# Attention and a spectral gate on one core: fewer sines, integer turns, first evacuations in halves, and a new order of work

## The chip, the cores and the metric

One core of one Trainium2 chip runs the whole program. The metric is the time on the device in microseconds (us), taken as the median over runs of the same kernel. TensorE (PE) multiplies, VectorE (DVE) and ScalarE (ACT) move results out of PSUM and do elementwise work, GpSimd (POOL) does elementwise work on SBUF alone, and SyncE (SP) issues nearly all DMAs.

## The reference

Sliced to what matters; S = 768, D = 64, four batches, eight heads, so the second stage has 512 channels.

```python
scores = scale * np.matmul(q, k.transpose(0, 1, 3, 2))
full_mask = causal                      # heads 0, 2 and 6
stream_mask = causal & (is_sink | in_win)   # the other heads: 4 first keys, window of 64
...
a = np.exp(scores - max) ; a = a / (sum(a) + 1e-09)
x = heads joined(np.matmul(a, v))       # (4, 768, 512)

proj = x @ w_proj                       # three parts: x1, x2, x3
X2 = np.fft.rfft(x2, n=S, axis=1)
H = np.fft.rfft(filter_fft, n=S, axis=0)[None, :, :]
x2_conv = np.fft.irfft(X2 * H, n=S, axis=1)
y = x1 * x2_conv * x3
return (y @ w_out)
```

## The kernel before

**Work units.** The 32 (batch, head) pairs are handled two heads at a time, as 16 pairs numbered n; pairs 4b to 4b+3 make batch b. A pair's causal score matrix has 21 blocks of 128x128. `CHUNKS` (L19) groups them into six chunks; a chunk's scores for both heads fill one pair of PSUM banks, and one ScalarE instruction `ex{n}.{c}` (L593) takes the exponential of the whole chunk. There are four such pairs of banks (slots 0 to 3, the number behind `@` in the order); every matmul stage shares them.

**A pair's path.** `lq`, `lk`, `lv` load q, k, v (SP). `cq`, `ck` (L522) cast to bf16, `cv` (L531) and `vf` (L541) prepare v. For n < 6 PE transposes q and k (`T{n}.{a}`, L550; a is 0 for q, 1 for k) and `E{n}.{a}` (L555) copies the result to SBUF; for later pairs a DMA transposes (`T{n}`, L560). `sc` (L574) makes the scores, as two matmuls on 64 rows each, one a head, side by side on the array. For n < 4, apart from chunks 0 and 1 of pair 0, `sb` (L587) adds a mask bias through the identity; otherwise `mk` (L603) multiplies the exponentials with a mask on DVE. `at` (L612) multiplies with v; `rec` and `nm` normalise; `f0`, `f1` (L634) add and subtract the two halves of the sequence.

**The spectral part.** The Fourier transforms are matmuls with a table `G` of cosines and sines. With the halves folded, even and odd frequencies separate, and G has for each of them (r = 0, 1) three segments: 128 cosines, 128 sines, and a third segment with 64 cosines and 64 sines of the remaining frequencies. `S` (L640) transforms a pair's attention output, `Se` copies it out, `X` (L681) projects with the second third of w_proj, `Xe` copies out, `pa`, `pb`, `pc` multiply with the transformed filter `HAB` (made by `F`, L435, and `H`, L445 and L447), `c` (L742) transforms back with `Gi` (G transposed by a DMA), `ce` and `cv{b}.{cb}.{r}` (L753) put the two halves together. `x1`, `x3` (L717) are the other two projections, `xs` (L725) copies x1 out, `g` and `y` multiply, `o` (L769) multiplies with w_out, `oe` copies out, `st` stores.

**How G is made.** Before: `fcol` (two pieces of 128 frequencies, two of 64), `angle` = fcol * t/768, `turns` = angle plus a large constant (which rounds to whole turns in fp32), `wrap` = rounded turns minus angle, each once per m = 0, 1, 2 over 384 columns; `size` = absolute value; then `sin1`, `cos1` for the first two segments and `sin2`, `cos2` for the third.

**Order.** Nothing is scheduled by the compiler: `ORDER` (L34) is one list of all operations, and each engine executes its own operations in the list's order. A suffix `/v`, `/s`, `/p` says that a copy, cast, or add goes to DVE, ACT or POOL; `@0` to `@3` names the PSUM slot. The list's text is the only place where engines and slots are chosen, so a wait on one engine holds back all that stands behind it on that engine.

Of the kernel before, what the change touches and what calls it, by code (L numbers as in the profile page):

```python
# [9 lines left out]
FP32 = mybir.dt.float32  # L10
BF16 = mybir.dt.bfloat16
I32 = mybir.dt.int32
# [7 lines left out]
    [(0, 0), (0, 1), (0, 2), (0, 3)],  # L20
    [(4, 4), (4, 5), (0, 4), (0, 5)],
    [(1, 1), (1, 2), (1, 3), (1, 4)],
    [(3, 3), (3, 4), (3, 5)],
# [23 lines left out]
sc3.0@3 sc3.3@2 f02/v sb3.0 vf3/v sb3.3 ex3.0 T4.1@0 scales T4.0 F2.0 ck5/p E4.1/v ex3.3 S2.0@3 cq6/p H2.2/s
E4.0/v S2.1 at3.1@2 H2.0/s Se2/v tn2@0 at3.0 H2.1/s te2/v cv4/p sc4.1@3 rec3 lq7 sc4.2@0 nm3 F0.1@1 ex4.2
F0.0 f03/v ex4.1 f13/v tn3@0 cq5/v T5.1@2 H0.0/v T5.0 S3.0@3 te3/v E5.0/s S3.1 H0.2/v E5.1/s x10.0.0@0
H0.1/v Se3/s x10.0.1 H0.3/v x10.1.0@2 H0.4/v xs0.0/s cv5/p lv6 kinds sc4.3@3 sc4.0@1 ex4.3 sc5.1@0 x10.1.1  # L50
ex4.0 mask1 x30.0.0@3 xs0.1/v lk8 ex5.1 x30.0.1 mask0 sc4.5@2 g0.0 sc4.4@1 ex4.5 X0.1.0@0 ex4.4 mask2 mk4.1
sc5.0@3 sc5.2@2 ex5.0 sc5.4@1 mk4.0 X0.1.1 mask6 ex5.2 x10.3.1@3 Xe0.1/v vf5/s x10.3.0 ck6/p F1.1@2 xs0.3/v
ex5.4 F1.0 T6 mask3 sc5.5@3 vf4/v H1.0/s sc5.3@1 cq7/p x30.1.0@0 mk4.2 lq8 ex5.5 x30.1.1 lv7 ex5.3 X0.2.1@3
mk5.2 H1.1/s at4.1@1 mk5.0 H1.2/s X0.2.0 ck7/s mk5.1 g0.1 cv6/s at4.0 T7 Xe0.2/s at5.1@2 mask4 vf6/p rec4
at5.0 nm4 ck8/s sc6.4@3 rec5 sc6.2@0 f04/v ex6.4 lq9 x10.2.0@1 nm5 x10.2.1 lk9 ex6.2 mask7 mask5 sc6.5@2
cq8/p sc6.1@3 xs0.2/v ex6.5 x30.2.0@0 ex6.1 f15/p mk6.2 sc6.0@1 sc6.3@2 T8 x30.2.1 ex6.0 X0.0.0@3 f05/v
ex6.3 g0.2 sc7.3@1 sc7.1@2 mk6.0 ex7.3 sc7.5@0 X0.0.1 mk6.1 ex7.5 tn4 f14/v S4.0@1 ex7.1 cv7/v sc7.4@0
Xe0.0/v tn5 vf7/p S4.1 ex7.4 S5.1@2 Se4/v cq9/p sc7.0@3 sc7.2@0 ex7.0 S5.0 ck9/v at6.1@1 mk7.2 ex7.2 T9
at6.0 mk7.0 Se5/s sc8.4@3 mk7.1 sc8.0@0 hB ex8.0 rec6 at7.0@2 sw0.1 nm6 sw0.0 at7.1 ex8.4 hA f06/v f16/p
sc8.5@0 lv8 sc8.3@1 rec7 ex8.5 S6.0@3 tn6 nm7 ex8.3 sc8.2@0 S6.1 f17/v ex8.2 f07/v tn7 S7.1@1 Se6/v S7.0  # L60
pa0.1 sc9.2@0 Se7/s sc9.4@3 lk11 sc9.0@2 pa0.0 ex9.2 X1.1.1@1 mk8.2 Gi ex9.4 pb0.1 X1.1.0 pc0.1 ex9.0
X1.0.0@0 mk8.1 X1.2.1@3 Xe1.1/s lq10 pa0.2 cv8/v sc8.1@2 sc9.1@1 pb0.2 vf8/p ex8.1 X1.2.0 pc0.2 X1.0.1 lk10
Xe1.2/s x11.1.1@2 ex9.1 mk8.0 x31.1.1@3 pb0.0 ck11/p x11.1.0 mk9.0 lq11 x31.1.0 xs1.1/s at8.1@1 Xe1.0/s g1.1
at8.0 x11.0.0@2 pc0.0 lv9 rec8 x11.0.1 nm8 x31.0.1@3 xs1.0/v f18/p lv10 sc9.5@1 sc9.3@0 ex9.5 x31.0.0 f08/p
cq10/s c0.1.0@1 g1.0 x11.2.1@2 ex9.3 c0.1.1 ck10/s mk9.1 c0.0.0@0 ce0.1/s mk9.2 T10 x11.2.0 cq11/p ce0.0/s
cv0.1.0 c0.3.1@3 xs1.2/s cv0.1.1 c0.3.0 T11 y0.1 x31.2.1@1 cv9/p ce0.3/v x31.2.0 cv0.3.0 vf9/p lv11 S8.1@2
g1.2 lq12 S8.0 c0.0.1 cv10/p cv0.3.1 Se8/s at9.1@1 cv0.0.0 lwo y0.3 sc10.3@2 sc10.2@3 ex10.3 cv0.0.1 at9.0
lk12 vf10/v ex10.2 x30.3.1@0 rec9 nm9 sc10.4@2 sc10.0@3 ex10.4 x30.3.0 y0.0 f19/p c0.2.0@1 ex10.0 g0.3 tn8
c0.2.1 f09/p sc10.5@2 ce0.2/v sc11.4@3 ex10.5 S9.1@0 cv0.2.0 ex11.4 cv11/p S9.0 tn9 cv0.2.1 x11.3.0@2 pa1.1
Se9/s sc11.5@3 y0.2 lk13 sc11.3@1 ex11.5 x11.3.1 vf11/v ex11.3 sc11.1@3 mk11.2 sc10.1@0 ex11.1 o0.1.0@1  # L70
# [12 lines left out]
ck15/s x12.2.0 nm13 o1.1.0@3 T15 xs2.2/s pa2.2 sc14.3@1 sc14.0@0 mk14.2 sc14.2@2 ex14.0 o1.0.0 sw2.0 cv15/v
pb2.1 o1.0.1 ex14.2 o1.1.1 x32.2.1@0 oe1.1/v cv14/p ex14.3 x32.2.0 vf15/p o1.4.0@2 vf14/s st1.1 g2.2 tn13
# [30 lines left out]
def kernel(  # L115
# [13 lines left out]
    nc = tc.nc  # L129
# [709 lines left out]
```

## Time and profile before

| | before |
|---|---|
| runs, us | 199.34, 198.08, 197.48, 197.08, 196.9 (median 197.48) |
| the profiled execution's own time | 199.34 us, its span 197.6 us |
| PE busy | 184.4 us (93%), 1725 instructions |
| DVE busy | 173.1 us (88%), 300 instructions |
| ACT busy | 143.3 us (73%), 183 instructions |
| POOL busy | 46.6 us (24%), 68 instructions |
| granted TensorE clock, mean | 0.988 |
| DMA | 37.31 MB, mean 189 GB/s |

The span is the time from the first to the last profiled instruction. A matmul's row includes the time in which its last columns drain, and the next matmul runs in that time too: consecutive 512-column matmuls start about 0.216 us apart (16 of them take 3.45 us in the chain) but have rows of 0.379 us on average. "Idle" of PE in the profile is counted from the end of such a row, so a wait costs the array about 0.17 us more than its idle time.

### The profile page before, as it was taken

What the parts mean: (1) busy time and instruction counts of PE and PEld (TensorE: products, weight loads), DVE (VectorE), ACT (ScalarE), POOL (GpSimd) and SP (SyncE); (2) the same over time, 40 slices, a digit from 0 to 9 for tenths busy, and PEclk for the clock granted to TensorE, in tenths of its full rate; (3) what the DMA queues carried; (4) which work ended last, traced back from release to release, by engine and by line L of the source; (5) the groups of instructions that cost most, each with busy time, mean ns of one, the idle gap of its engine ahead of it and who ended that gap; (6) DMA issues with size and microseconds to landing.
All of it is one profiled execution on the core that took longest, in us unless ns stands there. A gap on an engine that the chain in (4) does not pass through costs nothing.

```text
span 197.6 us, 4335 instructions
## 1 busy us (share of the span) xinstructions
PE 184.4 (93%) x1725; PEld 104.5 (53%) x1740; DVE 173.1 (88%) x300; ACT 143.3 (73%) x183; POOL 46.6 (24%) x68
## 2 busy tenths in 40 slices
PE   7489989999998999999998999999989999999990
PEld 2236656764473474465643744466537654555540
DVE  7788999898999999998997898989899986968950
ACT  4969998989998898848388769689879524422341
POOL 4243673333023320415731210322030000000000
PEclk9979999999999999999999999999999999999998
DMA  5999999999989968999999789998998221302346
GB/s 172 305 261 314 252 335 213 228 190 233 194 139 205 165 126 178 205 229 214 194 190 185 128 205 231 216 226 212 230 234 258 43 40 36 126 2 88 124 168 257
DMA packets 93782, 37.31 MB, mean 189 GB/s; under 512 B 84162, under 2 KB 89282, under 8 KB 93762
## 3 DMA queue, kind: packets, MB, share of 16 engines
q1 hardware_dynamic: 91650, 34.94, 80.4%
q0 software_dynamic: 2112, 2.10, 6.6%
q8 instruction: 13, 0.21, 0.5%
q14 instruction: 7, 0.06, 0.1%
HBM read 24.64 MB, written 6.29 MB: 157 GB/s over the span
## 4 chain that ended last, share of the span: by engine, by line
PE 60%; DVE 14%; DMA 12%; ACT 7%; issue 2%; POOL 1%; SPq 1%; ACTq 0%; DVEq 0%; POOLq 0%
PE x_ps L717 14%; PE X_ps L681 10%; PE out_ps L769 8%; PE sc L574 6%; PE att L612 6%; DMA qk_f<-in_k_dram 6%; PE S_ps L640 6%; PE c_ps L742 5%; ACT pT L593 4%; DMA v_f<-in_v_dram 4%; DMA qkT<-qk_bf 2%; DVE conv L753 2%; PE sc L587 2%; PE F_ps L435 2%; DVE attn L627 1%
## 5 line engine op out<-in xcount | busy, mean ns | idle before, releaser
L593 ACT ACTIVATE pT<-sc 128x1024 bf16<-128x1024 f32 (+2 forms) x96 | 82.2, 918 | 12.2 <-PE sc L574 9.6
L717 PE MATMUL x_ps<-xT,wproj 128*128 128x384 bf16 x256 | 46.3, 326 | 0.0
L717 PEld LDWEIGHTS <-wproj 128*128 128x128 bf16 x256 | 24.0, 98 | 18.1 <-issue 2.0
L574 PE MATMUL sc<-qkT 64*128 64x512 bf16 (+3 forms) x256 | 27.6, 312 | 2.4 <-DVE x1s L180 1.1
L603 DVE TENSOR_TENSOR pT<-pT,mask 128x1024 bf16<-128x1024 bf16 x37 | 24.9, 700 | 1.1 <-ACT pT L593 1.1
L612 PEld LDWEIGHTS <-pT 128*128 128x128 bf16 x672 | 22.8, 97 | 3.7 <-issue 1.4
L612 PE MATMUL att<-v_aug,pT 128*128 128x65 bf16 x352 | 23.9, 193 | 0.2
L769 PE MATMUL out_ps<-wout,gy 128*128 128x512 bf16 x89 | 23.1, 380 | 0.5 <-DMA wout<-in_moe_w_out_dram 0.2
L681 PE MATMUL X_ps<-wproj,spectrum 128*128 128x512 bf16 x90 | 22.2, 379 | 0.5
L612 PE MATMUL att<-v_far,pT 128*128 128x65 bf16 x320 | 20.7, 193 | 0.0
L574 PEld LDWEIGHTS <-qkT 64*128 64x128 bf16 x256 | 10.3, 94 | 17.1 <-issue 11.8
L742 PE MATMUL c_ps<-Gi,P 128*128 128x384 bf16 x96 | 18.9, 326 | 0.0
L640 PE MATMUL S_ps<-G,halves 128*128 128x384 bf16 x96 | 18.4, 326 | 0.2
L753 DVE TENSOR_TENSOR conv<-evs,c_ps 128x384 bf16<-128x384 f32 x32 | 16.6, 549 | 1.3 <-ACT evs L184 1.0
L182 POOL CAST v_aug<-v_f 128x768 bf16<-128x768 f32 x10 | 8.5, 853 | 36.1 <-DMA v_f<-in_v_dram 36.1
L541 POOL TENSOR_TENSOR v_far<-v_aug,vmask 128x520 bf16<-128x520 bf16 x9 | 10.2, 1133 | 25.0 <-DVE v_aug L180 16.1
L627 DVE TENSOR_TENSOR attn<-att,rec 128x768 bf16<-128x768 f32 x16 | 15.3, 955 | 0.7
L184 ACT COPY o<-out_ps 128x1024 f32<-128x1024 f32 (+1 forms) x10 | 8.9, 886 | 9.3 <-PE out_ps L769 6.9
L182 POOL CAST qk_bf<-qk_f 128x768 bf16<-128x768 f32 x13 | 11.5, 889 | 14.3 <-DMA qk_f<-in_k_dram 10.7
L184 ACT CAST spectrum<-S_ps 128x768 bf16<-128x768 f32 x11 | 8.8, 804 | 8.3 <-PE S_ps L640 8.1
L769 PEld LDWEIGHTS <-gy 128*128 128x128 bf16 x96 | 8.9, 98 | 10.8 <-issue 1.5
L681 PEld LDWEIGHTS <-spectrum 128*128 128x128 bf16 x96 | 8.9, 98 | 10.7 <-issue 1.3
(98 smaller groups left out, 251.3 us busy)
## 6 DMA issues: line engine op xcount, KB each, us to landing
qk_f<-in_q_dram SPq DMA_DIRECT2D x16, 384.0 KB, 5.7
qk_f<-in_k_dram SPq DMA_DIRECT2D x16, 384.0 KB, 5.9
v_f<-in_v_dram SPq DMA_DIRECT2D x16, 384.0 KB, 6.5
out_dram<-o SPq DMA_DIRECT2D x9, 512.0 KB, 3.3
filt<-in_moe_filter_fft_dram SPq DMA_DIRECT2D x1, 1536.0 KB, 9.4
wproj<-in_moe_w_proj_dram POOLq DMA_DIRECT2D x3, 512.0 KB, 9.4
out_dram<-o SPq DMA_DIRECT2D x6, 256.0 KB, 2.5
Xw<-X SPq DMA_DIRECT2D x8, 128.0 KB, 2.6
```

What stands on the lines that cost most here:

```text
L182: nc.gpsimd.tensor_copy(out=out, in_=in_)
L184: nc.scalar.copy(out=out, in_=in_)
L574: nc.tensor.matmul(sc[:, hh, m * 128:(m + cnt) * 128], lhsT=qkT(n)[rows, 1, j * 128:(j + 1) * 128], rhs=qkT(n)[rows, 0, i * 128:(i + cnt) ...
L593: nc.scalar.activation(out=pT(n)[:, :, c, 0:w], in_=held[f"sc.{n}.{c}"][:, :, 0:w], func=AF.Exp, scale=SCALE)
L603: nc.vector.tensor_mul(near, near, which)
L612: nc.tensor.matmul(att[:, hh, 65 * i:65 * i + 65], lhsT=pT(n)[:, hh, c, 128 * m:128 * m + 128], rhs=(v_far(n) if i >= j + 2 else v_aug(n)) ...
L640: nc.tensor.matmul(ps[:, r, 0:HS], lhsT=halves(n)[:, r, m, :], rhs=G()[:, r, m].rearrange("p s f -> p (s f)"), start=(m == 0), stop=(m == ...
L681: nc.tensor.matmul(ps[:, u, :], lhsT=spectrum(b)[:, cc, r, seg * 128:seg * 128 + 128], rhs=wproj()[:, cc, DM:2 * DM], start=(cc == 0), sto ...
L717: nc.tensor.matmul(ps[:, s, 0:HS], lhsT=wproj()[:, cc, part * DM + cb * 128:part * DM + (cb + 1) * 128], rhs=xT(b)[:, cc, s * HS:s * HS + HS],
L742: nc.tensor.matmul(ps[:, r, 0:HS], lhsT=P(b)[:, t, u, ch], rhs=Gi()[:, r, :, seg, :], start=(seg == 0), stop=(seg == 2))
L753: fn(conv[:, half * HS:half * HS + HS], held[f"evs.{b}.{cb}"], held[f"c_ps.{b}.{cb}"][:, 1, 0:HS])
L769: nc.tensor.matmul(ps[:, i % 2, :], lhsT=gy(b)[:, cb, i * 128:(i + 1) * 128], rhs=wout()[:, cb, :], start=(cb == 0), stop=(cb == NC - 1))
```

## The change

1. **Sines.** `fcol`, `turns`, `angle` and `size` shrink from 384 to 256 columns. `sin2` and `cos2` go. The third segment of G is now copied from the first two, in reversed order and with the sign of the position's parity: four operations `far{p}{r}` on DVE, and one operation `signs` (two small POOL instructions) that they read.
2. **Turns.** `angle{m}` goes; `turns{m}` multiplies and writes an int32 tile (the write rounds), and `wrap{m}` multiplies again and subtracts it.
3. **First pair.** `E0.0` and `E0.1` become two halves each (64 of the 128 positions a half, that is the first and the second 384 rows of the sequence).
4. **Chunks.** Block (0, 3) moves from the first chunk to the fourth: the first has three blocks, the fourth four.
5. **Order.** `ORDER` is replaced as a whole: 1001 operations become 1003, and engines, slots and positions are chosen anew.

```diff
 CHUNKS = [
-    [(0, 0), (0, 1), (0, 2), (0, 3)],
+    [(0, 0), (0, 1), (0, 2)],
     [(4, 4), (4, 5), (0, 4), (0, 5)],
     [(1, 1), (1, 2), (1, 3), (1, 4)],
-    [(3, 3), (3, 4), (3, 5)],
+    [(3, 3), (3, 4), (3, 5), (0, 3)],
...
-    turns = C("turns", [128, NM, HS], FP32, "P")
+    turns = C("turns", [128, NM, 256], I32, "P")
...
-        @op(f"angle{m}")
-            vp().tensor_scalar(out=angle()[:, m], in0=fcol(), scalar1=tfrac()[:, m:m + 1], scalar2=None, op0=ALU.mult)
         @op(f"turns{m}")
-            vp().tensor_scalar(out=turns()[:, m], in0=angle()[:, m], scalar1=MAGIC, scalar2=None, op0=ALU.add)
+            vp().tensor_scalar(out=turns()[:, m], in0=fcol(), scalar1=tfrac()[:, m:m + 1], scalar2=None, op0=ALU.mult)
         @op(f"wrap{m}")
-            nc.vector.scalar_tensor_tensor(out=angle()[:, m], in0=turns()[:, m], scalar=MAGIC,
-                                           in1=angle()[:, m], op0=ALU.subtract, op1=ALU.subtract)
+            nc.vector.scalar_tensor_tensor(out=angle()[:, m], in0=fcol(), scalar=tfrac()[:, m:m + 1],
+                                           in1=turns()[:, m], op0=ALU.mult, op1=ALU.subtract)
...
+    @op("signs")
+        for p in range(2):
+            nc.gpsimd.tensor_scalar(out=signs()[:, p:p + 1], in0=par(), scalar1=4.0 * p - 2.0, scalar2=1.0 - 2.0 * p,
+                                    op0=ALU.mult, op1=ALU.add)
+    for p in range(2):
+        for r in range(2):
+            @op(f"far{p}{r}")
+                near = G()[:, r, :, p, 1:65] if r == 0 else G()[:, r, :, p, 0:64]
+                vp().tensor_scalar(out=G()[:, r, :, 2, 64 * p:64 * p + 64], in0=near[:, :, ::-1],
+                                   scalar1=signs()[:, p:p + 1], scalar2=None, op0=ALU.mult)
...
-                @op(f"E{n}.{a}")
-                    copy(qkT(n)[:, a].rearrange("d (p t) -> d p t", t=NT),
-                       held[turned(n, a)][:, a, 0:S].rearrange("d (t p) -> d p t", t=NT))
+                for half in range(2 if n == 0 else 1):
+                    @op(f"E{n}.{a}.{half}" if n == 0 else f"E{n}.{a}")
+                        rows = slice(64 * half, 64 * half + 64) if n == 0 else slice(0, 128)
+                        copy(qkT(n)[:, a].rearrange("d (p t) -> d p t", t=NT)[:, rows],
+                             held[turned(n, a)][:, a, 0:S].rearrange("d (t p) -> d p t", t=NT)[:, rows])
```

The opening of the new order, and two later pieces that the prediction speaks of:

```
mblank fcol0 lk0 tcol quarter table blank0@0 fcol1 tfrac lq0 ident turns1/v lret turns2/v par sin0 lk1
turns0/v wrap2 lq1 wrap0 lq2 wrap1 lk2 sin1 size ck0.1/p lv0 ck0.0/v blank1@1 cos1 lv2 ones0 heads0 T0.1@0
cq0.1/v cq0.0/s parb code0 E0.1.0/s T0.0@1 ck1/p unit E0.1.1/s blank2@2 E0.0.0/v code1 heads1@0 E0.0.1/v
T1.1@3 lk3 sc0.0@2 heads2 sc0.4@1 E1.1/v code2 sc0.1@0 ex0.0 bias0 ex0.1 sc0.5@3 bias1 sc0.3@2 cq1/v sb0.3
sb0.4 bias2 ex0.3 T1.0@0 mask01 mask00 sb0.5 ck2/p E1.0/v lq3 ex0.4 sc0.2@2 lv1 sb0.2 signs bias3 sc1.5@0
lfilt ex0.2 sc1.1@1 vmask sb1.1 cq2/v sb1.5 ex0.5 mk0.0 sc1.4@2 lq4 sb1.4 ex1.1 cv0/v sc1.2@3 sb1.2 bias6
far10/v ex1.5 sc1.3@1 bias4 bias5 ex1.2 T2.0@0 vf0/v sb1.3 ck3/p T2.1 far00/v lk4 ex1.4 at0.1@3 lv3 cq3/p
...
x30.2.1 lk9 f14/v mk5.2 ex6.5 sc6.4@1 lq9 sc6.2@0 vf7/v ex6.4 at5.1@3 ck8/p g0.2 at5.0 ex6.2 sc6.0@1 rec5
...
```

How many operations change engine between the two lists (DVE, ACT, POOL in each line: before, then after):

| operation | DVE | ACT | POOL |
|---|---|---|---|
| `xs` (x1 out of PSUM) | 6, 1 | 10, 15 | |
| `ce` (first half of the inverse) | 8, 6 | 8, 10 | |
| `oe` (output) | 5, 3 | 10, 12 | |
| `Xe` | 2, 4 | 10, 8 | |
| `Se` | 5, 4 | 11, 12 | |
| `E` (q, k transposed; the first pair's are halves after) | 9, 7 | 3, 7 | |
| `f0`, `f1` | 23, 20 | | 9, 12 |
| `ck` | 5, 3 | 6, 2 | 6, 12 |
| `cv` (cast of v) | 5, 2 | 1, 5 | 10, 9 |
| `vf` | 5, 5 | 2, 1 | 9, 10 |
| `te` | 3, 4 | 1, 0 | |

## The prediction

> **What bounds the kernel now.** I read the busy times and the slices first, then the stretches, the chain, and last the waits of PE.
>
> ```profile
> PE 184.4 (93%) x1725; PEld 104.5 (53%) x1740; DVE 173.1 (88%) x300; ACT 143.3 (73%) x183; POOL 46.6 (24%) x68
> PE   7489989999998999999998999999989999999990
> PEclk9979999999999999999999999999999999999998
> ```
>
> PE is busy in every slice from the third to the last but one. The slice with clock 7 is the exception: from 12.05 to 15.47 us the granted clock was one half. The chain says the same: from 9.64 us on it is mostly PE, and PE's last matmul ends at 193.2. So the end is PE's own work from 9.64 on, plus the places where PE starts a matmul later than it could. Adding up matmuls in the order of the list (columns at the spacing that free stretches show: 0.216 us for 512, 0.163 for 384, 0.031 for 65) and comparing with their real starts, PE is 8.8 us behind its own work at 15.5 us, 9.2 at 22.9, 10.5 at 39, 12.9 at 107.5 and 14.6 at the end. The opening costs 8.8 us, and all the rest only 5.8.
>
> ```profile
> 8.76 0.82 POOL L182 CAST qk_bf<-qk_f 128x768 bf16<-128x768 f32 x1 [5.49 <-DMA qk_f<-in_k_dram]
> 9.64 0.51 PE L550 MATMUL qkT_ps<-identity,qk_bf 128*128 128x128 bf16 x6 [2.29 <-POOL qk_bf L182]
> 11.90 0.69 PE L587 MATMUL sc<-bias,identity 128*128 128x128 bf16 x4 [0.81 <-DVE bias L396]
> 10.62 1.02 ACT L593 ACTIVATE pT<-sc 128x1024 bf16<-128x1024 f32 x1 [0.91 <-PE sc L574]
> 12.21 1.51 ACT L593 ACTIVATE pT<-sc 128x512 bf16<-128x512 f32 x2 [0.56 <-PE sc L587]
> 14.24 5.20 ACT L593 ACTIVATE pT<-sc 128x768 bf16<-128x768 f32 x6 [0.52 <-PE sc L587]
> ```
>
> The first scores wait in PE's queue behind T1.1, which waits for the second pair's k. Then the second and fourth exponentials wait for the mask bias.
>
> ```profile
> PE sc L574 <- DVE x1s L180: 1.1, 2, 0.7
> PE sc L574 <- DVE xT L180: 0.7, 1, 0.7
> PE sc L574 <- DMA qkT<-qk_bf: 0.5, 1, 0.5
> 39.35 1.46 PE L435 MATMUL F_ps<-fold,G 128*128 128x512 bf16 x5 [0.25 <-ACT HAB L447]
> ```
>
> These are five later waits (columns of the first three: idle in all, times, longest; the fourth is an instruction with its idle). Measured from start to start, so with the 0.17 us of overlap that each loses, they cost 0.82 and 0.60 (x1s at 63.2 and 107.5), 0.83 (xT at 28.9), 0.67 (qkT at 145.9) and 0.41 (39.35): 3.3 of the 5.8 us.
>
> **The sines and turns.** Before: three passes of 384 columns, some 0.33 to 0.47 us apart, then four sines on ACT (0.85, 0.51, 0.60, 0.92). After: turns and wraps of 256 columns, six instead of nine, and two sines. On DVE that saves some 1.6 us before 6 us, on ACT 1.1. Both at zero: behind them T1.1 still waits for lk1, fourth in SP's list before and after, which landed at 8.71. Nothing reads G before the first transform at 25 us. Without that cover they would be worth up to 1.7 us (the table load ahead of the first exponential ended at 9.71 and could end near 8.0). Added are four `far` on DVE; the nearest rows, 128x128 in 0.175 us and 128x384 in 0.35, give 0.7 to 1.4 us in all, in a stretch (15 to 25 us) where DVE has 9.2 of 10 us busy. I take 1.0; `cv0`, `vf0` and `nm0` stand behind them, and the walk below pays for it. `signs` is two POOL instructions: between 0.12 us (a small memset) and 1.71 (L342, the only arithmetic of POOL on the int32 tile), so 0.2 to 3.4. I take 3.4. POOL is busy only 1.9 of the 5 us from 15 to 20; queued behind are ck3, cq3 and cv1, which by the upper price end at 17, 18 and 19 us, and T3 and at1 come at 19.7 and 22. Hidden; uncovered it is 1 to 2 us.
>
> **Halves and chunks.** E0.0 and E0.1 took 0.95 each, in series on DVE, done at 8.72; now two engines share them and the first scores need only the first halves. Hidden by the same T1.1; zero. The first exponential is 0.82 instead of 1.02, the fourth chunk's the reverse; zero in sum. The fourth chunk's scores become two runs. In a run of scores the next pair of another width starts 9 ns late, so 16 more pairs cost 0.15 us.
>
> **The opening, walked by hand.** Behind T1.1 (9.64 again) the list puts two chunks that need no bias. ex0.0 starts at 10.4, ex0.1 follows at 11.2 and covers the wait for code2, heads2 and the bias: sb0.3 runs at 11.8, ex0.3 at 12.2, and ACT has no more gaps (before: 0.56 and 0.52). Following PE, DVE (0.95 for E1.1 and E1.0, 0.27 a bias, 0.69 mk0.0 and vf0) and ACT (0.93 for 1024 columns) to the first `at`, it starts at 18.05 us after 9.9 us of listed work, against 17.75 after 8.8. That is 8.15 behind instead of 8.9: **-0.75 us**. If PE is granted half clock from 12 to 15.5 again, it and not ACT sets the pace there and -0.3 is left; with k1 late by 1 us, +0.5. If the clock stays full in both, -1.0.
>
> **Switches between scores and other matmuls.** This speaks against the change, and is easily overlooked, since columns and matmuls otherwise stay.
>
> ```profile
> 16.69 0.50 PE L587 MATMUL sc<-bias,identity 128*128 128x128 bf16 x4
> 17.13 0.39 PE L574 MATMUL sc<-qkT 64*128 64x512 bf16 x2
> 17.45 0.39 PE L587 MATMUL sc<-bias,identity 128*128 128x256 bf16 x2
> ```
>
> The scores at 17.13 use 64 rows each, side by side, so 512 columns take 0.216 us; the next matmul on 128 rows starts 0.32 after them, 0.1 late. Four bias matmuls before them need 0.33 and the scores start 0.44 later. Over the trace the median is 95 ns on leaving and 98 on entering: 0.193 a visit. The list before visits scores 46 times, the new one 52. Two of the six fall into the opening, which other waits pace; four cost 0.8: **+0.8 us** (0 if they fall into waits, 1.2 at most).
>
> The Trainium skill, TensorEngine Tiling (Array Packing), Key Properties, says that a change of tiling mode drains TensorE, while changing the tile within a mode does not; it names no price, and the rows above agree with it on both halves.
>
> **What leaves DVE.** Counting engine changes with the page's means (xs 0.95 against 0.80, ce 0.55 and 0.48, oe and Xe 1.21 and 1.02, f 0.45 against 0.96 on POOL, casts 0.55 to 0.59 against 0.84 to 0.89), DVE loses 12.4 us, ACT gains 3.5, POOL 8.5. ACT has room (73%). For the five waits I looked up what now stands between producer and user in the list. x1s of 63.2 and 107.5 goes to ACT behind one or two exponentials, with 1.8 and 2.2 us of matmuls to cover it. te0 no longer stands behind f11 and f01 (the pair took 1.92 us) but behind fold1, with 0.65 to spare. H2.2 moves to DVE, and the bank's next user comes 4.7 us after its matmuls; the evictions and what ACT does between them take 3.3. T15 has 6.1 us of matmuls from its place to its first score, instead of 4.1. All five go: **-3.3 us**.
>
> Others will form; the list is new everywhere. Over the whole list, the reuses of a PSUM slot whose cover (matmuls between the slot's last use and its next) exceeds its eviction by under 0.3 us number 47 in the old list and 44 in the new, so neither is looser there. DMA transposes have 4.4 us at least, where 4.1 was late and 4.5 was not. Bounds: nothing new, and 5.8 anew, all that PE lost after the opening. As DVE has 12 us more room, I take half of what was removed: **+1.6 us**.
>
> POOL's work costs DVE something. `halves` at 26.48 (f11 and f01) shows it: f11 alone took 1.65 us beside POOL's v_far, against 0.35. Over all groups DVE's rows exceed their undisturbed times by 7.1 us, 0.15 for each us of POOL; 8.5 more makes 1.3, so DVE's relief is 11 and not 12.4. That is inside the +1.6.
>
> SBUF — State Buffer, Who interferes with whom, speaks harder against it: a DVE instruction with two SBUF inputs and a GpSimd instruction that reads SBUF exclude each other, and the second waits for the first to end. An estimate by that page: if each of ten added POOL instructions blocked one of DVE for its whole 0.9 us, 9 of the 12.4 us would be gone, the waits would come back in full, and the sum would be about +0.2. This trace shows one full block (f11) and many POOL instructions without, so the measured share decides.
>
> **Sum.** -0.75 + 0.8 + 0.15 - 3.3 + 1.6 = -1.5 us. The profiled execution took 199.34 us, 1.74 of them outside its span of 197.6, and is the slowest of the five; the same sum there gives 197.8. Against the median of 197.48 it is **196.0**.
>
> **Rivals.**
> 1. *All of it holds and nothing new forms*: -3.1, with the full clock -3.35: 194.2. For it: DVE's relief. Against: the nearly equal number of tight slots.
> 2. *The waits only move*: +3.3 in place of +1.6 makes +0.2: 197.7. For it: PE is at 97% between 20 and 160 us, so any list leaves a few us.
> 3. *DMA transposes come late* (slower). The stretch is pairs 8 to 14: T8, T9, T10, T12 and T14 have 5.1 to 5.3 and 4.4 us to their scores, the transposes' median from issue to landing is 4.7, single ones need more, and SP's one queue holds back all behind a wait. If they land 1 us later than before, four are late by 0.5 to 1 us and the loads behind them too: +3.5 on top of rival 2's +0.2: 201.2; from 0.7 us later on it decides (199.5). For it: DMA engines are near full until 155 us. Against: T15's only loss before was 0.67.
> 4. *The opening doesn't move* (half clock, k1 later): -1.5 + 0.75 to +1.25 = 196.7 to 197.2.
>
> **How the numbers follow.** My case (195.0 to 197.0) 0.40, rival 1 0.20, rival 2 0.13, rival 3 0.20, rival 4 0.07. A change of 1% (195.5 and 199.5) is about what a measurement of this kernel can tell from none. Faster by more: rival 1 and about half of my case, 0.41. Slower by more: rival 3 and a bit of rival 2, 0.22. Within: 0.37. The range runs from rival 1's end, 194.0, to 199.6, where rival 3 begins to decide; my case's own is 195.0 to 197.0.
>
> **What would show it.** Right: ex0.0 near 10.4 and no gap on ACT before 16 us; DVE near 160 us busy, POOL near 58; no PE wait on x1s at all; 52 visits of scores; PE's idle sum smaller though its work is 1 us more. Wrong: lk1 landing elsewhere than 8.7; new PE waits of over 3 us in sum, on ACT's xs or on qkT; many DVE rows stretched beside POOL; the clock halved for longer.

## The result, and the profile after

The new kernel is slower: 201.02 us median over 43 runs (198.29 to 207.75), the old one 197.67 over 80 (196.44 to 201.25). The ratio is 1.0097, 95% interval 1.0078 to 1.0116. This ratio, like every ratio below, leaves out slow executions, those more than 1.5% above the same kernel's fastest; for the new kernel these are 19 of the 43, all from 201.3 us up, so its median, 1.7% above the old one, holds a loss that the ratio does not. Forecast were 196.0 us and a range of 194.0 to 199.6.

The profiled execution took 203.48 us, 201.7 of them its span. Its busy times, PE's slices and its granted clock:

```profile
PE 186.9 (93%) x1756; PEld 105.0 (52%) x1772; DVE 165.8 (82%) x284; ACT 147.6 (73%) x188; POOL 58.4 (29%) x77
PE   7987998999999999999759999999989999999990
PEclk9999999999999999999996999999999999999999
```

DVE is 7.3 us less busy than before, ACT 4.3 and POOL 11.8 us more. PE's row is full as before, except for a hole in slices 20 and 21 (5 us a slice, so from 96 to 106 us), and behind it the clock drops for one slice. The hole is named by PE's waits (us in all, times, longest):

```profile
PE sc L580 <- DMA qkT<-qk_bf: 4.1, 3, 2.2
PE att L618 <- DVE v_far L545: 1.1, 1, 1.1
PE sc L580 <- DVE qkT L180: 0.9, 2, 0.5
PE S_ps L646 <- DVE qkT L180: 0.5, 1, 0.5
PE att L618 <- DVE xT L180: 0.4, 1, 0.4
```

Nothing waits for x1s any more. In its place stand scores that wait for the DMA transpose of q and k, and four waits that the old kernel did not have or had elsewhere. The timeline shows the first line's two great instances, with the issue of w_out's load by POOL ahead of them (start, duration, what, idle before and releaser), then the chain with the transposes in it, then two windows with the granted clock:

```profile
95.41 0.81 POOL L423 DMA_DIRECT2D wout<-in_moe_w_out_dram  x1
99.30 0.56 PE L580 MATMUL sc<-qkT 64*128 64x384 bf16 x6 [1.33 <-DMA qkT<-qk_bf]
105.26 0.39 PE L580 MATMUL sc<-qkT 64*128 64x384 bf16 x4 [2.21 <-DMA qkT<-qk_bf]
```

```profile
95.35 9.86 DMA qkT<-qk_bf
105.21 0.05 issue
...
142.69 6.94 DMA qkT<-qk_bf
```

```profile
99.00:105.20 6.20, 3.74 (x29) 1.56 (x29) 3.46 (x6) 4.11 (x5) 2.98 (x3) 1.00 1.38 158
105.20:109.20 4.00, 3.94 (x19) 1.25 (x20) 2.52 (x4) 2.30 (x3) 1.10 (x1) 0.57 1.37 221
```

T11, the transpose of pair 11, was issued at 95.35 and took 9.86 us to land; in the execution profiled before it took 4.2 us (94.82 to 99.02). In these window rows the first numbers are the length and PE's busy time, and the 0.57 near the end is the granted clock: after the wait PE ran for some 3.4 us at half clock (3.4 of 4.0 us at a half and the rest at full make 0.57). The Trainium skill, TensorE: Matmul & The Clock Gate, Part 1: The HAM clock gate, gives about 3.4 us as the window in which PE's idleness is judged. The half clock lasts as long here (3.41 us, from 105.70 on), but PE's longest idle time ahead of it was 2.2 us, shorter than that window.

w_out's load was issued at 95.41, 0.06 us after T11, and landed at 106.22. In the old list `lwo` stands on POOL behind `cv9`, `vf9` and `cv10`; in the new list these casts have moved away and only `cq11` and `cv11` stand ahead. So it starts 1.3 us sooner, at T11's own time.

The opening of the new kernel, and of one that has the old order up to 93 us (before_lwo_with_T11, below):

```profile
6.91 0.82 POOL L182 CAST qk_bf<-qk_f 128x768 bf16<-128x768 f32 x1 [1.83 <-DMA qk_f<-in_k_dram]
8.61 9.12 ACT L599 ACTIVATE pT<-sc 128x768 bf16<-128x768 f32 x11
15.97 1.32 DVE L545 TENSOR_TENSOR v_far<-v_aug,vmask 128x520 bf16<-128x520 bf16 x1
17.33 0.19 PE L618 MATMUL att<-v_far,pT 128*128 128x65 bf16 x1 [1.13 <-DVE v_far L545]
```

```profile
7.36 0.82 POOL L182 CAST qk_bf<-qk_f 128x768 bf16<-128x768 f32 x1 [4.08 <-DMA qk_f<-in_k_dram]
9.75 5.10 ACT L593 ACTIVATE pT<-sc 128x1024 bf16<-128x1024 f32 x6
15.36 0.68 DVE L541 TENSOR_TENSOR v_far<-v_aug,vmask 128x520 bf16<-128x520 bf16 x1
15.85 0.25 PE L612 MATMUL att<-v_aug,pT 128*128 128x65 bf16 x3
```

The second pair's k lands at 6.9 and 7.3 us here, not at the 8.71 of the execution that the prediction was made from. The new order's first exponential comes 1.70 us after k's cast begins (8.61 and 6.91) and ACT has no gap in 9.12 us, both as foretold; but the first product with v begins at 15.95 us, no sooner than the old order's 15.85. By the prediction's listed work (9.9 us ahead of it against 8.8) PE is 6.1 us behind there and not 7.0, with k cast 0.45 us sooner; then it waits for `vf0`, 1.3 us from start to start, and at 23 us it is 7.4 us behind in both profiles.

### The profile page after: what moved, and what is told of

It is laid out like the page before. It is cut to its first block, busy times and chain, and to the rows that moved or that the text cites. A ratio compares the mean times of both kernels' runs of the same rounds, so it can differ in the third digit from the quotient of the medians.

```text
span 201.7 us, 4388 instructions
## 1 busy us (share of the span) xinstructions
PE 186.9 (93%) x1756; PEld 105.0 (52%) x1772; DVE 165.8 (82%) x284; ACT 147.6 (73%) x188; POOL 58.4 (29%) x77
## 4 chain that ended last, share of the span: by engine, by line
PE 63%; DMA 13%; DVE 10%; ACT 5%; SPq 3%; issue 2%; POOL 2%; POOLq 0%; DVEq 0%
PE x_ps L723 17%; PE X_ps L687 10%; PE out_ps L775 9%; DMA qkT<-qk_bf 8%; PE att L618 7%; PE sc L580 7%; PE c_ps L748 6%; PE S_ps L646 4%; ACT pT L599 3%; DMA v_f<-in_v_dram 3%; DMA qk_f<-in_k_dram 2%; PE sc L593 2%; DVE bias L400 1%; PE F_ps L439 1%; DVE v_far L545 1%
## 5 line engine op out<-in xcount | busy, mean ns | idle before, releaser
L723 PE MATMUL x_ps<-xT,wproj 128*128 128x384 bf16 x256 | 47.4, 330 | 0.0
L580 PE MATMUL sc<-qkT 64*128 64x128 bf16 (+3 forms) x288 | 28.3, 293 | 5.4 <-DMA qkT<-qk_bf 4.1
L609 DVE TENSOR_TENSOR pT<-pT,mask 128x1024 bf16<-128x1024 bf16 x37 | 28.5, 784 | 2.5 <-ACT pT L599 2.5
L182 POOL CAST qk_bf<-qk_f 128x768 bf16<-128x768 f32 (+1 forms) x19 | 18.8, 1001 | 32.3 <-DMA qk_f<-in_k_dram 18.1
L640 POOL TENSOR_TENSOR halves<-attn 128x384 bf16<-128x384 bf16 x12 | 12.4, 1042 | 33.0 <-DVE attn L633 33.0
L646 PE MATMUL S_ps<-G,halves 128*128 128x384 bf16 x96 | 19.3, 332 | 0.6 <-DVE qkT L180 0.5
L545 POOL TENSOR_TENSOR v_far<-v_aug,vmask 128x520 bf16<-128x520 bf16 x10 | 11.6, 1160 | 20.8 <-ACT v_aug L184 17.8
L184 ACT COPY o<-out_ps 128x1024 f32<-128x1024 f32 (+1 forms) x12 | 10.5, 880 | 7.2 <-PE out_ps L775 7.2
L737 DVE TENSOR_TENSOR gy<-x1s,x_ps 128x768 bf16<-128x768 bf16 x12 | 11.3, 949 | 4.8 <-PE x_ps L723 2.4
L184 ACT CAST x1s<-x_ps 128x768 bf16<-128x768 f32 x15 | 11.9, 806 | 4.3 <-PE x_ps L723 4.3
```

What stands on the lines that cost most here:

```text
L182: nc.gpsimd.tensor_copy(out=out, in_=in_)
L184: nc.scalar.copy(out=out, in_=in_)
L580: nc.tensor.matmul(sc[:, hh, m * 128:(m + cnt) * 128], lhsT=qkT(n)[rows, 1, j * 128:(j + 1) * 128], rhs=qkT(n)[rows, 0, i * 128:(i + cnt) ...
L609: nc.vector.tensor_mul(near, near, which)
L646: nc.tensor.matmul(ps[:, r, 0:HS], lhsT=halves(n)[:, r, m, :], rhs=G()[:, r, m].rearrange("p s f -> p (s f)"), start=(m == 0), stop=(m == ...
L723: nc.tensor.matmul(ps[:, s, 0:HS], lhsT=wproj()[:, cc, part * DM + cb * 128:part * DM + (cb + 1) * 128], rhs=xT(b)[:, cc, s * HS:s * HS + HS],
```

## The experiments

Several kernels were timed beside the same runs of the old one. Its medians were 198.05 us beside after_again, after_lwo_early, before_lwo_with_T11 and open_after_rest_before; 197.88 beside before_17_visits, before_new_code, before_four_moves and open_after_rest_before2; 197.87 beside after_47_visits, after_47_vf0_early, before_new_sines and before_new_chunks; 197.94 beside the other three. "Lag" is PE's start less the work listed ahead of it, as in the prediction, each visit to the 64-row scores counted with its 0.193 us.

### w_out's load out of the way, or into it

The new kernel again, then the same with `lwo` moved up behind `cq9`; and the old list with `lwo` at T11's time.

```diff
  (new list)  ... mk7.2 ex7.1 sc7.0@2 cq9/p
+ lwo
  ... cv11/p g1.2 S8.0@2 lk12
- lwo
```
```diff
  (old list)  ... c0.3.0 T11 y0.1 x31.2.1@1 cv9/p
+ lwo
  ce0.3/v ... cv10/p cv0.3.1 Se8/s at9.1@1 cv0.0.0
- lwo
```

> The changed kernel once more, for a second profile. In the first one (span 201.7 us) PE stood still for 1.5 us at 99.3 and 2.4 us at 105.3, each time for a DMA transpose of q and k (T10, T11): T11 was issued at 95.35 us and landed at 105.21, while the load of w_out was issued at 95.41. Theory A (w_out's load overtakes T11 on the shared DMA engines): the waits vary with the race between the two; in an execution near 198.5 us the T11 wait is under 1 us, in one above 201 it is 2 us or more. Rival B (the new order loses evenly: switches between scores and other matmuls, waits on DVE and ACT): the wait for T11 is alike in fast and slow executions, and the difference is spread over many places.

> The changed kernel with one word of the order moved: the load of w_out (lwo) follows cq9 on POOL, some 28 us earlier than before. Theory A: T11 lands 4 to 5 us after its issue, the waits at 99 and 105 us shrink to under 1 us in sum, the time falls by 2 to 4 us to 196.5 to 198.5, and the spread of the runs becomes like that of the kernel before (some 2 us instead of 9). Rival B: time and spread stay within 0.5 us of the changed kernel's, about 199.5 to 201.

> The kernel before with one word of the order moved: lwo goes ahead of vf9 and cv10 on POOL, so that it is issued near 95 us, with T11, and not at 96.7. Theory A: T11 lands 8 to 10 us after its issue instead of 4.2, PE waits 2 us or more for the scores of pair 11, and the time rises by 1 to 4 us, with a wide spread. Rival B: nothing but w_out's own arrival changes; within 0.5 us of the kernel before.

Measured: the new kernel 203.98 us (199.18 to 205.5, ratio 1.010 with 1.004 to 1.016); with the early load 200.11 (199.3 to 201.16, 1.0114 with 1.0076 to 1.0152); a second time 200.68 (197.99 to 201.19, 1.0095 with 1.005 to 1.0139). The old list with the load at T11's time took 199.22 (197.15 to 204.15, 1.0027 with 0.9993 to 1.006); five of its twelve runs lie between 200.25 and 204.15, where the old kernel's 17 end at 198.85.

> The kernel of after_lwo_early once more, beside the one with the old chunks. If what is left over before is PE's own work for the six added visits (1.17 us in the order's sum, against waits that are level with before): 199.0 to 200.2, ratio 1.006 to 1.012. If it is waits: PE's lag on its own work at the end differs from the first profile's 12.95 us by more than 1 us, and the ratio goes with it.

PE's waits on the transposes, first new kernel again, then with the early load, first and second profile:

```profile
PE sc L580 <- DMA qkT<-qk_bf: 3.9, 2, 2.9
```
```profile
PE sc L580 <- DMA qkT<-qk_bf: 0.3, 1, 0.3
```
```profile
PE sc L580 <- DMA qkT<-qk_bf: 2.1, 2, 1.2
PE c_ps L748 <- DMA Gi<-G: 0.6, 1, 0.6
```

And the old list, where the load beside T11 makes a chain step of it:

```profile
93.06 7.72 DMA qkT<-qk_bf
```

From issue to landing, in nine of the profiles, in us (a star where w_out's load was issued within 1.3 us of it):

| kernel | pair 9's transpose (T9) | T11 | w_out's load issued |
|---|---|---|---|
| before | 3.7 | 4.2 | 96.70 |
| before_new_sines | 3.7 | 4.1 | 95.70 |
| before_17_visits | 3.7 | 4.1 | 96.40 |
| before_lwo_with_T11 | 3.7 | 7.7* | 93.31 |
| before_four_moves | 8.1* | 4.3 | 65.92 |
| after | 3.7 | 9.9* | 95.41 |
| after_again | 3.8 | 11.0* | 94.87 |
| after_lwo_early | 9.0* | 5.2 | 67.03 |
| after_lwo_early_again | 7.7* | 5.2 | 67.11 |

Where T11 took 4.1 or 4.2 us the load was in flight too, but issued 1.9 us or more behind it (1.7 in open_after_rest_before2, where T11 took 3.9). Issued up to 0.3 us behind a transpose, or up to 1.3 ahead of it, the load doubles it, whichever transpose it meets, in both lists. In the new list T9, with the early load, lands nearly in time (at 76.11 in the first profile, its first score starts at 76.15, 0.4 us late); T11, with the later load beside it, does not. So this part is shown: the collision made the new kernel's spread (up to 207.75 us, at most 201.19 in the 18 runs with the early load). How much of the median it makes is less certain: 3.9 us with six runs each (203.98 less 200.11), but the 201.02 of all 43 runs is only 0.3 to 0.9 above the two medians with the early load. The 1% of the ratio stays with the early load. That load is not clear of the transposes, though: it meets T9 in both profiles, which cost PE 0.4 us in the first, and no run of the new list had it clear of both. So what part of the 1% is still w_out's load is open.

### Old and new halves of the list joined

The new list as far as `tn3`, then the old. In the first version pair 5's k was loaded behind pair 6's, as the new list has it, while the old rest needs it first.

```diff
  (new list to tn3, then the old)  second version:
- ... at0.0 E2.1/v ex1.3 sc1.0@2 ones2 lk6 ... F2.1@3 lk5
+ ... at0.0 E2.1/v ex1.3 sc1.0@2 ones2 lk5 ... F2.1@3 lk6
```

> The new order up to tn3 (about 37 us), then the old order for the rest, with all of the change's code (sines, integer turns, halves, chunks). If the opening is a gain that the rest gives back (theory A, and the opening of the first profile, where the first attention matmuls start at 15.95 us instead of 17.75): 1 to 2 us faster than the kernel before, 195.5 to 196.5. If the code changes or the opening are at fault (rival C): as slow as the changed kernel, 199 to 201. If the gain of the opening is used up by DMA, since loads come no earlier: within 0.5 us of the kernel before.

> The new order up to tn3, then the old one, as in open_after_rest_before, but with the loads of pair 5's and pair 6's k exchanged: in that run PE waited 4.5 us at 43.5 us for pair 5's k, which the new order loads after pair 6's and the old order needs early. With the seam mended, if the new opening gains nothing (its first attention matmul at 16 us, the same as the old order's where the second pair's k lands at 7.3 us): within 0.8 us of the kernel before. If the new opening gains: 1 to 2 us faster. If it costs: 1 us slower or more, with PE's waits before 40 us.

Measured: 204.74 us (201.2 to 208.04), with PE waiting 4.5 us at 43.5 us for that k, an artefact of the seam that tells nothing; then 200.28 (198.76 to 201.91), ratio 1.0105 with 1.0062 to 1.0147. In the second profile k landed at 8.19 us. An opening worth -0.75 in an unchanged rest would have given 197.1. But the new chunks are in this old rest as well, where they alone cost 1.6 us (below): pair 13's transpose takes 6.4 us here and PE waits 1.25 us for it at 131.49. Beside before_new_code, which has the same code with the old opening, it is 0.9 us faster (200.28 and 201.21), with intervals that overlap. With the seam and the late k also in the number, it shows no gain of the opening and excludes none; what tells of the opening is the lag in the profiles above.

### Visits of the 64-row scores

Seventeen more visits in the old list, by moving 18 matmul words between the last two chunks of a group (three of the 18 shown); later, five fewer in the new one, by moving five words beside their other halves.

```diff
  (old list)
- sc5.1@0 x10.1.1 ... sc7.2@0 ex7.0 S5.0 ... sc13.4@0 cv13/p at12.0
+ x10.1.1 sc5.1@0 ... S5.0 sc7.2@0 ex7.0 ... at12.0 sc13.4@0 cv13/p
```
```diff
  (new list, lwo behind cq9)
- sc7.1@0 S4.0    S5.0@1 ... sc7.2@2 S5.1    S9.0@0 ... sc11.3@3 S9.1    x11.3.0@1 ... x11.3.1
+ S4.0 sc7.1@0    sc7.2@2 S5.0@1 S5.1    S9.0@0 S9.1 ... sc11.3@3    x11.3.0@1 x11.3.1
- x30.3.1@3 ... sc10.3@2 x30.3.0
+ x30.3.1@3 x30.3.0 ... sc10.3@2
```

> The kernel before with 18 words moved: behind pair 3, a matmul stage that follows a group of scores is put between the group's last two chunks, so that PE visits the 64-row scores 63 times instead of 46. The same matmuls, banks and engines. Theory S (each visit costs PE 0.19 us, and PE is the bound, so the change's six more visits cost what is left of its loss without the transposes' delay, 1.2 us): 17 more visits cost 3.3 us, 200.5 to 202 beside 198. Theory W (the switches fall into PE's waits, since other engines hold it up anyway): under 0.8 us.

> The new kernel with w_out's load moved up behind cq9 (as in after_lwo_early, whose time was 200.11 us and 1.0114 of before), and with five matmul words moved next to their other halves (S4.0, S5.0, S9.1, x11.3.1, x30.3.0), so that PE visits the 64-row scores 47 times and not 52. Theory A, the visits cost their switches: 18 words moved in the old order cost 2.3 to 2.4 us for 17 visits more, 0.14 us each; five fewer give -0.7 us: about 199.4, ratio 1.008, and the work of PE in the order's own sum falls by about 0.9. Theory B, the visits are hidden by waits of other engines, and what the 17 cost was their changed evictions: no change, 200.1, ratio 1.011. Theory C, a word moved from its place breaks its cover: 0.5 to 1 us slower, with a new PE wait on S4, S5, S9 or x11.3 in the trace.

Measured: 17 more visits take 200.15 us, ratio 1.0121 (1.0103 to 1.0139): 0.0121 x 197.88 = 2.4 us, 0.14 us a visit. Six come to 0.85 us, against the 0.8 of the prediction. Five fewer in the new list did not give the 0.7 back: 200.8 us, 1.0131 (1.0085 to 1.0177). Its waits, which all stand in the profile of after_47_vf0_early as well, name what stood in the way:

```profile
PE sc L580 <- ACT pT L599: 1.4, 4, 0.7
PE xt_ps L659 <- DVE attn L633: 1.0, 1, 1.0
PE sc L580 <- DVE X L180: 0.8, 1, 0.8
```

Where two chunks of scores more stand in a row, PE reaches the bank that ACT's exponential still holds: this wait was 0.3 us, once, in the profile with 52 visits. In the old list a visit costs its switches; in the new one the stage that PE visits from also covers the exponentials, and the price of its visits alone was not measured there.

### Each code change by itself, in the old list

All code changes at once, with `signs` and `far` in places of mine between 17 and 23 us; then sines and turns alone, chunks alone, halves alone.

```diff
  (old list)
- angle0/v angle1/v angle2/v sin2 cos2   E0.0/v   E0.1/v
+ E0.0.0/v E0.0.1/v   E0.1.0/v E0.1.1/v
+ signs (behind cq3)  far10/v (bias6)  far00/v (cv1)  far01/v (f00)  far11/v (E3.1)
```

> All of the change's code (256 columns, integer turns, sines copied, halves, chunks) in the old order; signs and the four far put at their earliest places, the rest unmoved. Theory A (the code is neutral, the loss is in the new order): within 0.8 us of the kernel before. Rival C (the code itself costs, by far and signs in the full stretch from 15 to 25 us, or by two-run chunks): 1 to 2 us slower, with DVE behind from 16 us on. Rival G (the code itself gains, and the order lost more than that): 0.8 us faster or more.

> The old order, chunks and first evacuations, with the sines and turns of the change alone: six passes of 256 columns in place of nine of 384, two sines in place of four, signs on POOL and four far on DVE between 17 and 23 us, where DVE is full. All code changes together cost 3.3 us in the old order (201.21, ratio 1.0164). Theory A, the sines are what costs it (far delay qkT of the third pair, attn and the normalisation behind them, which waited 0.7 to 1.2 us at 16.3, 23.2 and 27.3 us): +2 to +3.3 us, ratio 1.010 to 1.016. Theory B, the prediction's: far 1.0 us on DVE against 1.1 to 1.6 us less work ahead of 6 us, all hidden: within 0.5 us of before, ratio 0.998 to 1.003.

> The old order and sines, with block (0, 3) moved from the first chunk to the fourth, and nothing else. For every pair the first exponential is 0.2 us shorter and the fourth 0.2 us longer, and the fourth chunk's scores become two runs. Theory A, the prediction's: 16 more pairs of matmuls cost 0.15 us: ratio 1.000 to 1.002. Theory B, the old order was laid out for a short fourth chunk (sc3 stands late in most pairs, ahead of the product with v): the exponential that is 0.2 us longer is waited for in each of 16 pairs, up to 0.1 to 0.2 us each: +1.5 to +3 us, ratio 1.008 to 1.015. If both before_new_sines and this one stay under 1.004, the halves of the first pair (two instructions in place of one on DVE) are left as the cause, or the 3.3 us are a sum of waits that need all three edits.

> The old order, chunks and sines, with the first pair's two evacuations in two halves each, all on DVE. In the old order the sines alone cost 0.95 us and the chunks alone 1.43 us by the medians (0.8 and 1.6 by the ratios), all code changes together 3.3. Theory A, the halves cost the rest: two more DVE instructions in series ahead of the first scores, +0.2 to +0.9 us, ratio 1.001 to 1.004. Theory B, T1.1's wait for the second pair's k covers them, as the prediction has it: ratio 0.998 to 1.002, and the 3.3 us hold about 0.9 that only the three together make.

| in the old list | median, us | ratio (interval) |
|---|---|---|
| all code changes | 201.21 | 1.0164 (1.0128 to 1.0201) |
| sines and turns | 198.82 | 1.0041 (1.0009 to 1.0073) |
| chunks | 199.30 | 1.0083 (1.0058 to 1.0109) |
| halves | 198.14 | 1.0021 (0.9988 to 1.0055) |

The three add up to 1.45% of the 1.64%, which is inside the intervals. The chunks are the largest, though the array's work is the same. Of their 1.6 us the profile shows this wait in the timeline, and the step of the chain ahead of it:

```profile
128.85 0.72 PE L574 MATMUL sc<-qkT 64*128 64x384 bf16 x10 [1.39 <-DMA qkT<-qk_bf]
```
```profile
122.24 6.56 DMA qkT<-qk_bf
```

This is pair 13's transpose. With the new chunks in the old list it takes 6.4 to 6.7 us in all four profiles that have them, 4.7 to 5.1 in the six that don't. Why a fourth exponential that is 0.2 us longer lengthens this transfer was not found. Then the same edit undone in the new list:

```diff
  (new list, lwo behind cq9)
-    [(0, 0), (0, 1), (0, 2)],
+    [(0, 0), (0, 1), (0, 2), (0, 3)],
-    [(3, 3), (3, 4), (3, 5), (0, 3)],
+    [(3, 3), (3, 4), (3, 5)],
```

> The new kernel with w_out's load behind cq9, and block (0, 3) back in the first chunk. In the old order moving that block alone cost 1.6 us (199.30, ratio 1.0083), and its trace showed 1.56 us of it as one wait of PE for the DMA transpose of pair 13. Theory A, the chunks carry a price of their own in any list: about 1.6 us less than after_lwo_early, 198.5, ratio 1.003. Theory B, the price was the old list's, which was laid out for the old chunks, and the new list is laid out for the new: no gain, 200.1 or up to 1.5 us more, ratio 1.011 to 1.019, with new waits in the opening, where the first exponential now needs the second halves of the first pair's evacuations.

Measured: 201.76 us (199.64 to 204.01), ratio 1.0165 (1.0109 to 1.0222), beside 1.0095 with the new chunks. So the same edit costs 0.8% in the old list, and in the new one it saves about 0.7%, with intervals that overlap. The chunks have no price that holds in both lists, and undoing them does not bring back what remains of the loss.

### Taking waits away

Three of the prediction's five waits (the two on x1s and the one on xT), treated in the old list by three moves, with w_out's load moved up as the fourth; and `vf0` ahead in the new one.

```diff
  (old list)
- xs0.2/v   xs1.3/v   f11/v tn0@3 ex2.3 lv5 f01/v sb2.0 te0/v   cv0.0.0 lwo
+ xs0.2/s   xs1.3/s   tn0@3 te0/v f11/v ex2.3 lv5 f01/v sb2.0   cq9 lwo
```
```diff
  (new list, lwo behind cq9, 47 visits)
- cv0/v sc1.2@3 sb1.2 bias6 far10/v ex1.5 sc1.3@1 bias4 bias5 ex1.2 T2.0@0 vf0/v
+ cv0/v vf0/v sc1.2@3 sb1.2 bias6 far10/v ex1.5 sc1.3@1 bias4 bias5 ex1.2 T2.0@0
```

> The kernel before with five words changed: w_out's load after cq9 instead of after cv10; te0 (and tn0) ahead of f11 and f01 on DVE; xs0.2 and xs1.3 on ACT. It takes away the waits that the prediction had counted (xT 0.8 to 1.1 us, x1s 0.8 and 0.6 us) and w_out's transfer from the stretch of T10 and T11. If waits add up on PE: 1.5 to 2.5 us faster than the kernel before, 195.5 to 196.5. If they only move, as they did in the changed kernel: within 0.6 us.

> As after_47_visits, and vf0 stands directly behind cv0 on DVE, ahead of bias6, far10, bias4 and bias5. In the new kernel the first matmul on v waited 1.1 to 1.4 us for vf0 (start to start), which the prediction had not seen. Theory A, the opening's delay is carried to the end: 1.3 us less than after_47_visits, about 198.1 and level with before. Theory B, waits only move: something a few us later (E2.1, the third pair's scores, xT at 33 us or qkT at 35 us) waits instead; within 0.4 us of after_47_visits. Under B PE's lag on its own work at 35 us is again about 8.7 us; under A it is about 7.4.

Measured: the four moves take 199.08 us, ratio 1.0046 (1.0026 to 1.0066). Of the waits on xT and x1s (1.09 and 0.72 us in before_lwo_with_T11) 0.35 is left. All of PE's waits from 14 to 75 us, with the four moves and then in before_lwo_with_T11 (the old order up to there):

```profile
PE sc L574 <- ACT pT L593: 0.3, 1, 0.3
PE F_ps L435 <- ACT HAB L447: 0.2, 1, 0.2
PE sc L574 <- DVE qkT L180: 0.2, 1, 0.2
```
```profile
PE sc L574 <- DVE xT L180: 0.9, 1, 0.9
PE sc L574 <- DVE x1s L180: 0.6, 1, 0.6
PE F_ps L435 <- ACT HAB L447: 0.2, 1, 0.2
PE sc L574 <- DVE qkT L180: 0.2, 1, 0.2
```

So up to 75 us most of what was removed stayed away: from 23 to 74 us PE's lag grows by 1.7 us with the four moves (7.1 to 8.8), by 2.8 in before_lwo_with_T11 (7.4 to 10.3), and by 2.6 to 2.9 in four other profiles of the old order with the old chunks. Then this came:

```profile
65.92 0.80 POOL L419 DMA_DIRECT2D wout<-in_moe_w_out_dram  x1
...
75.42 0.82 PE L574 MATMUL sc<-qkT 64*128 64x512 bf16 x6 [2.01 <-DMA qkT<-qk_bf]
```

w_out's load, moved up, now meets T9, and in the old list T9 has no room. PE waits 2.0 us for it, the clock is granted at a half from 76.74 to 80.15, and at 80 us the lag is 12.7, beside 10.5 in before_lwo_with_T11. In this profile the load that was moved in the same edit costs more than the other three moves had gained; the 0.9 us in time hold both, and what the three are worth without it was not measured. `vf0` early: 201.03 us, beside 200.8 without it. The wait on v_far is gone from the profile, and PE's lag is the same 15 us later (9.0 and 8.7 us at 32 us), since other waits stand there instead:

```profile
20.09 0.29 PE L580 MATMUL sc<-qkT 64*128 64x128 bf16 x4 [0.66 <-ACT qkT L184]
...
32.21 0.51 PE L659 MATMUL xt_ps<-identity,attn 128*128 128x128 bf16 x6 [1.02 <-DVE attn L633]
```

k's cast began 0.2 us later in this profile (7.69 and 7.49), which is too little to account for a 1.3 us that didn't come.

## Why the prediction was wrong, point by point

**The opening, -0.75: failed.** Up to the first product with v the new order gains, as foretold; the lag at 23 us, 7.4 us in both lists, shows that nothing is left of it. One side of this is the old execution that the prediction was read from: it had k 1.4 us late and half clock from 12.05 to 15.47. In another profile of the same opening k lands at 7.3, the clock is full, and the first product with v starts at 15.85 instead of 17.75 us. (Of the seven other profiles of the old order one, before_new_halves, has such a half clock, from 11.77 to 15.18.) Over all profiles k's cast began between 6.6 and 8.8 us in the old list's opening, between 6.7 and 8.2 in the new one's. I took one execution's luck for the list's property, and the rival "the opening doesn't move" got 0.07. The other side is `vf0`, left out of the walk as a wait: it took 1.32 us, against 0.68, beside a POOL cast from 15.84 to 16.73, and PE waited for it. With `vf0` ahead the wait went and others took its place. The Trainium skill, SBUF — State Buffer, Who interferes with whom, says that a DVE instruction with two SBUF inputs contends with a GpSimd instruction that reads SBUF; this row agrees with it.

**Switches, +0.8: right,** by the old list's 0.14 us a visit, below the median of the rows (0.193). Two differences cancel in the sum, four visits at 0.193 there and six at 0.14 here; in the new list the price was not measured.

**Five waits removed, -3.3, and half of it given back, +1.6: this is the step that failed most.** The waits on x1s went, as foretold. But in the new list with the load out of the way, measured from start to start and after the opening, PE loses 0.52 on xT at 33.0, 0.63 on an evacuation of q and k at 35.2, 0.40 at 76.2, 0.86 on Gi at 88.6, 0.44 on attn at 99.2 and 0.48 on T15 at 145.6: 3.3 us. These are its rows (for the third, the profile names P; T9 landed at 76.11):

```profile
32.98 0.25 PE L618 MATMUL att<-v_aug,pT 128*128 128x65 bf16 x3 [0.36 <-DVE xT L180]
35.22 1.62 PE L646 MATMUL S_ps<-G,halves 128*128 128x384 bf16 x9 [0.47 <-DVE qkT L180]
76.15 0.82 PE L580 MATMUL sc<-qkT 64*128 64x512 bf16 x8 [0.23 <-DVE P L696]
88.62 1.15 PE L748 MATMUL c_ps<-Gi,P 128*128 128x384 bf16 x6 [0.69 <-DMA Gi<-G]
99.22 0.56 PE L580 MATMUL sc<-qkT 64*128 64x384 bf16 x6 [0.27 <-DVE attn L633]
145.56 0.66 PE L580 MATMUL sc<-qkT 64*128 64x512 bf16 x8 [0.31 <-DMA qkT<-qk_bf]
```

The old list's other profile has xT 1.09, HAB 0.41, x1s 0.72, T11 0.54 and T15 0.54: 3.3. So the five waits brought 0 and not -1.7: the new list has as much waiting in other places, which was rival 2, with 0.13. "DVE has 12 us more room" was no reason for taking half. Whether a removed wait must come back is another question, and the runs answer it both ways: `vf0`'s came back within 15 us, while in the old list 1.1 of the 1.8 us on xT and x1s stayed away for as long as that trace can be compared, to 75 us.

**DVE's relief, 11 us: too large.** It was 7.3 in the first profile; with the early load it is 10.0 and 8.2 (163.7 and 165.5 us busy, beside 173.7 in before_lwo_with_T11). Over all groups, DVE's rows exceed their undisturbed times by 10.5 us after and 7.1 before, 3.4 more and not the 1.3 of the prediction; in the first profile with the early load it is 8.5 beside 6.9 in before_lwo_with_T11, 1.6 more. Most of the 3.4 is in the mask products, 0.78 us on average against 0.70:

```profile
L609 DVE TENSOR_TENSOR pT<-pT,mask 128x1024 bf16<-128x1024 bf16 x37 | 28.5, 784 | 2.5 <-ACT pT L599 2.5
```

**DMA transposes, at most 0.20 for rival 3: the mechanism came, by another cause.** Rival 3 let them come late because they get less time in the list; T11's room was in fact enough for its 4.2 us. I had counted what casts left POOL and what they cost, but not that `lwo`, which issues a transfer from POOL's queue, moved up past them onto T11's start. It named neither T11 nor w_out, and its price, 201.2, met the median of 201.02 by a different sum. T15, which I had put among the waits that go because it has 6.1 us of matmuls instead of 4.1, takes 6.5 to 7.5 us in every profile of the new list and 4.1 to 6.0 in the old list's, so it stays late; here the rival's own mechanism holds.

**Chunks, +0.15: wrong as a number.** The array's spacing is as read, but in the old list the edit costs 1.6 us by waits, and in the new it saves about 1.4, with intervals that overlap.

**Sines, turns and halves, nothing:** halves nearly so (+0.2%, interval with zero). `signs` took 0.5 us and not 3.4, the four `far` 1.1. In the old list the sines still cost 0.4%, where `far` stands in a full stretch. Removing DVE and ACT work ahead of 6 us brought nothing that could be seen, as foretold.

**The sum again.** Opening 0 (with v_far's wait in it), later waits 3.3 for 3.3, switches +0.85 by the price measured in the old list: +0.85; both profiles with the early load lose more. The first profile with the early load has a span of 197.6, 1.5 above the 196.1 of before_lwo_with_T11; with the visits counted at 0.193 us, PE's lag at its end is 13.1 us beside 13.0 there, so little but the switches (1.2 us at that price) is lost in it. The second has 199.0, its added 1.4 being the scores that wait for T10 (1.39, where in the first they waited 0.44 for attn) and for T15 (1.03 for 0.48). In time the early load measures 1.0114 and 1.0095 of 197.9 to 198.05, +2.3 and +1.9, between those two profiles. So about 1 us of what is left I put down to transposes that come late in some executions; that is read from two profiles and not tested by a run. On top of it, in the median, comes T11's collision. What the new list loses in a run near 198.5 us with the load at T11 was not traced, as both its profiles (203.48 and 204.20 us) show the collision.

## What to carry to other kernels

Before pricing an engine change, write down what else stands on that engine's queue, and what each later instruction of that queue starts: a cast that leaves POOL moves a DMA, and the DMA can double another one. Read the opening from more than one execution before calling a delay the list's. In a kernel where one engine is at 97% and everything is ordered by hand, do not price a removed wait by its length or by half of it: one came back in full within 15 us, another (xT) stayed away for over 40, and a whole new list waited as long as the old. Price what changes that engine's own work, and change one thing at a time, since a DMA moved along with the waits hid what they were worth.

## What the runs showed of the hardware

- A DMA transpose of pair 9 or 11 takes 3.7 to 5.5 us alone and 7.5 to 11.0 us when w_out's 512 KB load from POOL's queue starts with it.
- The cast of the second pair's k, which waits for a load at the same place of the list, begins between 6.6 and 8.8 us from one execution to the next.
- The clock was granted at a half for 3.4 us after a PE wait of 2.2 us behind one of 1.3 us (first profile of the new kernel), after one of 2.9 us (second profile) and after one of 2.0 us (before_four_moves), and in neither of the profiles with the early load, where no wait after the opening is over 1.3 us; PE's lag grows by 1.5 us in the first (14.7 to 16.2).
